# Where a path that is not taken keeps its transfers: GpSimd's queue, and turns on TensorE

## The chip, the cores and the metric

The kernel runs on one core of a Trainium2 chip. The metric is the device time of one execution in microseconds (us), lower is better; the time given for a kernel is the median of its runs. A profile is one more execution, taken with the hardware profiler. It gives a *span*, from the first to the last instruction of the program, which is a little shorter than the device time of that same execution.

The engines are called TensorE (PE, with PEld for its weight loads), VectorE (DVE), ScalarE (ACT), GpSimd (POOL) and SyncE (SP). SyncE computes nothing here; it issues transfers. A name with a q (SPq, ACTq) in a profile means the engine's sequencer: branches, semaphore instructions, drains and the issuing of transfers.

## The reference

The inputs are q, k and v of 4 batches, 8 heads, 768 tokens and 64 channels, a small matrix sort_net of 8x8 for each head, and the weights of a gated block. Cut to what matters:

```python
for _ in range(5):                       # P is sort_net
    P = exp(P - max(P, axis=-1))
    P = P / (sum(P, axis=-1) + 1e-09)
    P = P / (sum(P, axis=-2) + 1e-09)
k_sorted = einsum('bhij,bhjcd->bhicd', P, k_blocks)   # 8 blocks of 96 tokens
v_sorted = einsum('bhij,bhjcd->bhicd', P, v_blocks)
scores = q_block @ k_sorted_block.T / sqrt(64)
attn = softmax(scores)
x = attn @ v_sorted_block                # all heads side by side: 4 x 768 x 512
h = relu(x @ w_in); u, v = halves of h
v_s = w_spatial @ layernorm(v) + b_spatial
out = (u * v_s) @ w_out                  # 4 x 768 x 512, float32
```

## The kernel before, in words

The program has two paths, one after the other. The **usual path** computes everything without the maxima of the reference and without the 1e-09. The **general path** computes all of it again, with the maxima and the small term, one batch after the other and without overlap. It runs only if the usual path met a value outside some bounds. With the inputs used here no value is outside.

The usual path is written as a list of small units (`ORDER`, L18 to L51): `L` loads a q, k or v of one batch, `SK` is one round of the normalisation, `KT` mixes and turns k, `VM` mixes v and `VC` (L415) moves it into blocks, `SC` and `AT` are the scores and the attention of one pair of heads, `XT` (L506) turns attention output on TensorE with four 96x96 transposes a head pair and a copy, `XD` (L497) does the same turn with one transfer that transposes, and so on to `OS` (L643) and `OJ` (L690), which store the output. The list is the order on every engine. The last stores are `OJ` units; each is one transfer on SyncE's queue.

Loads go through GpSimd's queue; `load_sort_net` (L183), `VC`, `XD`, `OS` and `OJ` go through SyncE's. A transfer on SyncE's queue signals one of eight semaphores in turn, each with its own count.

Near the end of the list, `CK` (L694) compares the smallest and largest row sums and column sums with the bounds, `CF` (L709) adds up what it found into one integer, and `LF` (L715) loads that integer into a register of every engine. The branch is the last thing in the program:

```python
with tc.If(st["beyond"] > 0, preferred_fallthrough_block=True, label="general"):
    general_path()
```

Every engine has this branch (L773) in its own list of instructions, behind its last usual unit. An engine that doesn't take the general path jumps over its instructions to a short block of its own. In that block it adds to its semaphores what the general path would have added, each time after waiting that the usual path's own counts are complete, and jumps to the end of the program. There (the line of the launch, L800) SyncE waits for every semaphore in use, twelve instructions with two waits each, and drains; then all engines meet twice, and the program ends.

`general_path` (L724) calls the same unit functions as the usual path, `u_VC`, `u_OS` and `u_XD` among them, so its transfers stand in the queues that those functions name. It uses no `OJ`.

Of the kernel before, what the change touches and what calls it, by code (L numbers as in the profile page):

```python
# [65 lines left out]
def kernel(  # L66
# [12 lines left out]
    nc = tc.nc  # L79

    B, H, S, D = q.shape
# [8 lines left out]
    KC = DM // 128  # L90
    FC = DH // 128
    HP = H // 2
# [12 lines left out]
    def ps_tile(n, dt=FP32):  # L105
        return psum.tile([128, 2, 512 if dt == FP32 else 1024], dt, name=f"ps{n}", tag=f"ps{n}")

    def copy(eng, out, in_):
        if eng == "A":
            nc.scalar.copy(out=out, in_=in_)  # L110
        else:
            nc.vector.tensor_copy(out=out, in_=in_)
# [9 lines left out]
    p_all = const.tile([BH, NB, NB], FP32, name="p_all")  # L122
# [27 lines left out]
    st = {}  # L150
# [30 lines left out]
            nc.gpsimd.dma_start(out=w_out_sb, in_=moe_w_out.rearrange("(fc p) n -> p fc n", p=128))  # L181

    def load_sort_net():  # L183
        nc.sync.dma_start(out=p_all, in_=sort_net.rearrange("b h i j -> (b h) i j"))

    def u_S0():
        load_sort_net()
# [37 lines left out]
    def u_SK(n, safe=False):  # L225
        n = int(n)
        rows, cols = (first[:, 0:NB], first[:, NB:2 * NB]) if n == 0 else (rowsum, colsum)
        over_rows = lambda x: x.to_broadcast([BH, NB, NB])
        over_cols = lambda x: _raw_ap(x, 0, [x.ap[0], [0, NB], x.ap[1]])
        if safe:  # L230
            nc.vector.reduce_max(out=rowsum, in_=p_all, axis=AX.X)
            nc.vector.tensor_sub(out=p_all, in0=p_all, in1=over_rows(rowsum))
        nc.scalar.activation(out=p_all, in_=p_all, func=AF.Exp)
        nc.vector.reduce_sum(out=rows, in_=p_all, axis=AX.X)
        if safe:
            nc.vector.tensor_scalar_add(out=rows, in0=rows, scalar1=1e-9)
        nc.vector.reciprocal(out=rowsum, in_=rows)
        nc.vector.tensor_mul(out=p_all, in0=p_all, in1=over_rows(rowsum))
        nc.vector.reduce_sum(out=cols, in_=p_all.rearrange("p i j -> p j i"), axis=AX.X)
        if safe:  # L240
            nc.vector.tensor_scalar_add(out=cols, in0=cols, scalar1=1e-9)
        nc.vector.reciprocal(out=colsum, in_=cols)
        to = p16.rearrange("p (i j) -> p i j", i=NB) if n == 4 else p_all
        nc.vector.tensor_mul(out=to, in0=p_all, in1=over_cols(colsum))
        if n == 4:
            nc.vector.transpose(out=p_t, in_=p16)

    def u_PR(ps):
        pr = ps_tile(ps)[:, 0, 0:NB * BH].rearrange("p (i y) -> p i y", i=NB)
        for i in range(NB):  # L250
            nc.tensor.matmul(
                pr[:, i, :], lhsT=spread[:, (i % NI) * NB:(i % NI + 1) * NB].rearrange("p j t -> p (j t)"),
                rhs=p_t[:, (i // NI) * BH:(i // NI + 1) * BH], start=True, stop=True,
            )
        st["pr"] = pr
# [6 lines left out]
    def u_P0(lo, hi):  # L262
        lo, hi = int(lo), int(hi)
        n, pr = hi - lo, st["pr"]
        nc.vector.tensor_mul(
            out=pd(0)[:, lo:hi].rearrange("p h (i t) -> p h i t", t=TB),
            in0=_raw_ap(mask16, 0, [mask16.ap[0], [0, n], [0, NB], [1, TB]]),
            in1=_raw_ap(pr, lo, [pr.ap[0], [1, n], [BH, NB], [0, TB]]),
        )

    def u_PC(eng):
        copy(eng, prep_sb, st["pr"])

    def u_PD(b, lo, hi):
        b, lo, hi = int(b), int(lo), int(hi)
        n = hi - lo
        nc.gpsimd.tensor_mul(
            out=pd(b)[:, lo:hi].rearrange("p h (i t) -> p h i t", t=TB),
            in0=_raw_ap(mask16, 0, [mask16.ap[0], [0, n], [0, NB], [1, TB]]),
            in1=_raw_ap(prep_sb, b * H + lo, [prep_sb.ap[0], [1, n], [BH, NB], [0, TB]]),  # L280
        )
# [44 lines left out]
    def u_QN(ps, eng, b, hp):  # L326

        b, hp = int(b), int(hp)
        t = ps_tile(ps).rearrange("p x c -> p (x c)")
        for g in range(G):  # L330
            for hh in range(2):
                nc.tensor.matmul(
                    t[hh * 64:hh * 64 + 64, g * 128:(g + 1) * 128],
                    lhsT=st["q", b][:, 2 * hp + hh, g * D:(g + 1) * D], rhs=ident,
                    start=True, stop=True,
                )
        natural(eng, q_tile(b)[:, hp * S:(hp + 1) * S], t)
# [47 lines left out]
    def u_KT(ps, eng, b, hp):  # L385
        mixed("k", "kT", ps, eng, int(b), int(hp))
# [14 lines left out]
    def u_VM(ps, eng, b, hp):  # L401
        b, hp = int(b), int(hp)
        t = ps_tile(ps)
        for hh in range(2):
            nc.tensor.matmul(
                t[:, hh, 0:G * D], lhsT=pd(b)[:, 2 * hp + hh, :], rhs=st["v", b][:, 2 * hp + hh, :],
                start=True, stop=True,
            )
        copy(
            eng,  # L410
            vm[:, :, 2 * hp:2 * hp + 2, 0:D].rearrange("p g h d -> p h g d"),
            t[:, :, 0:G * D].rearrange("p h (g d) -> p h g d", g=G),
        )

    def u_VC(b, lo, hi):  # L415
        b = int(b)
        for i in range(int(lo), int(hi)):
            nc.sync.dma_start(
                out=vb[b % 2][:, i].rearrange("c h d -> c (h d)"),
                in_=vm[i * TB:(i + 1) * TB].rearrange("t g h d -> t g (h d)"),  # L420
            )
# [75 lines left out]
    def u_XD(b, ih, lo=0, hi=4):  # L497
        b, ih, lo, hi = int(b), int(ih), int(lo), int(hi)
        if ("xT", b) not in st:
            st["xT", b] = att.tile([128, 2, KC, HW], BF16, name="xT", tag="xT", bufs=2)  # L500
        nc.sync.dma_start_transpose(
            out=st["xT", b][:, ih, lo:hi].rearrange("p k (i c) -> p (k i) c", i=NI),
            in_=st["x", b, ih][:, lo:hi].rearrange("p k i c -> p (k i c)"),
        )

    def u_XT(ps, eng, b, ih, lo):  # L506
        b, ih, lo = int(b), int(ih), int(lo)
        if ("xT", b) not in st:
            st["xT", b] = att.tile([128, 2, KC, HW], BF16, name="xT", tag="xT", bufs=2)
        t = ps_tile(ps, BF16)[:, 0, 0:2 * HW].rearrange("p (k i c) -> p k i c", k=2, i=NI)  # L510
        for k in range(2):
            for i in range(NI):
                nc.tensor.transpose(t[:, k, i, :], st["x", b, ih][:, lo + k, i, :], ident[0:BLK, 0:BLK])
        copy(eng, st["xT", b][:, ih, lo:lo + 2].rearrange("p k (i c) -> p k i c", i=NI), t)
# [125 lines left out]
            st["o", b, n0] = ld.tile([128, 3, DM], FP32, name="o_sb", tag="ld")[:, 0:2]  # L640
        copy(eng, st["o", b, n0][:, lo:hi], st["o_ps", b, n0][:, lo:hi])

    def u_OS(b, n0, lo=0, hi=2):  # L643
        b, n0, lo, hi = int(b), int(n0), int(lo), int(hi)
        nc.sync.dma_start(
            out=out[b].rearrange("(c p) n -> p c n", p=128)[:, n0 + lo:n0 + hi, :],
            in_=st["o", b, n0][:, lo:hi],
        )
# [38 lines left out]
        st["o1", b, n, c0] = ld.tile([128, 3, DM], FP32, name="o1_sb", tag="ld")[:, 0, 0:c1 - c0]  # L687
        copy(eng, st["o1", b, n, c0], st["o1_ps", b, n, c0])

    def u_OJ(b, n, c0, c1):  # L690
        b, n, c0, c1 = (int(x) for x in (b, n, c0, c1))
        nc.sync.dma_start(out=out[b, n * 128:(n + 1) * 128, c0:c1], in_=st["o1", b, n, c0])

    def u_CK():  # L694
        nc.vector.memset(bad, 0.0)
# [28 lines left out]
    def general_path():  # L724


        st.clear()
        load_sort_net()
        for n in range(5):
            u_SK(n, safe=True)  # L730
        u_PR(0)
        u_P0(0, 8)
        u_PC("A")
        for b in range(B):
            if b > 0:
                u_PD(b, 0, 8)
            for x in ("q", "k", "v"):
                u_L(x, b, 0, H)
            for hp in range(HP):
                u_VM(2, "A", b, hp)  # L740
            u_VC(b, 0, NB)
            for hp in range(HP):
                u_QN(2, "A", b, hp)
                u_KT(3, "D", b, hp)
                for ih in range(2):
                    u_SM(b, hp, ih)
                    u_AT(2, b, hp, ih)
            for ih in range(2):
                u_XD(b, ih, 0, HP)
            for n in range(0, G, 2):  # L750
                u_VP(n % 4, "A", b, n, n + 1)
                u_ST(b, n)
                u_ST(b, n + 1)
            u_LN(b, 0, G)
            for n in range(G):
                u_LA(b, n)
            for m in range(2):
                for ih in range(2):
                    u_UP(2 * m + ih, "A", b, m, ih)
            for mc in range(FC):  # L760
                u_SP(mc, b, mc)
                u_GT("D", b, mc)
            for n in range(0, G, 2):
                u_OP(n % 4, b, n)
                u_OE("A", b, n)
                u_OS(b, n)
# [38 lines left out]
```

## Time and profile before

| | us |
|---|---|
| median of 3 runs | 161.39 |
| lowest and highest run | 161.30, 161.57 |
| the profiled execution's own time | 161.53 |
| its span | 159.7 |
| TensorE busy | 147.6 |
| VectorE busy | 113.1 |
| ScalarE busy | 85.7 |
| GpSimd busy | 42.2 |

The granted TensorE clock was 0.996 of full speed over the span. Busy times count compute instructions alone; semaphore instructions, branches, drains and the issuing of transfers are not in them, and are seen only when a view is asked for their line. In such an answer a row is: line, sequencer, operation, how many, the duration in ns (smallest, median, largest), and the start of the first and of the last one, in us from the span's start.

### The profile page before, as it was taken

What the parts mean: (1) busy time and instruction counts of PE and PEld (TensorE: products, weight loads), DVE (VectorE), ACT (ScalarE), POOL (GpSimd) and SP (SyncE); (2) the same over time, 40 slices, a digit from 0 to 9 for tenths busy, and PEclk for the clock granted to TensorE, in tenths of its full rate; (3) what the DMA queues carried; (4) which work ended last, traced back from release to release, by engine and by line L of the source; (5) the groups of instructions that cost most, each with busy time, mean ns of one, the idle gap of its engine ahead of it and who ended that gap; (6) DMA issues with size and microseconds to landing.
All of it is one profiled execution on the core that took longest, in us unless ns stands there. A gap on an engine that the chain in (4) does not pass through costs nothing. (4 is left out here: it accounts for less than half of the span.)

```text
span 159.7 us, 3977 instructions
## 1 busy us (share of the span) xinstructions
PE 147.6 (92%) x1647; PEld 89.2 (56%) x1661; DVE 113.1 (71%) x261; ACT 85.7 (54%) x117; POOL 42.2 (26%) x46
## 2 busy tenths in 40 slices
PE   6997989999999999999999999999999999899840
PEld 2355867845686668556465654655655554455410
DVE  4786889638995679867838669897558956947620
ACT  3556799968889409478572446555432242340220
POOL 7942782292000034040000650210004440005300
PEclk9999999999999999999999999999999999999998
DMA  3999999999999999950000657300911377037253
GB/s 84 259 204 204 204 208 202 208 224 239 269 207 202 204 226 241 214 92 4 0 4 0 123 90 131 61 4 0 290 71 34 69 259 266 0 137 259 96 202 112
DMA packets 27526, 23.58 MB, mean 148 GB/s; under 512 B 7280, under 2 KB 24432, under 8 KB 27504
## 3 DMA queue, kind: packets, MB, share of 16 engines
q0 software_dynamic: 14352, 11.80, 46.6%
q1 hardware_dynamic: 13152, 11.49, 25.1%
q8 instruction: 14, 0.23, 0.6%
q14 instruction: 8, 0.07, 0.2%
HBM read 24.78 MB, written 6.29 MB: 195 GB/s over the span
## 5 line engine op out<-in xcount | busy, mean ns | idle before, releaser
L620 POOL TENSOR_TENSOR gt<-z,u_sb 128x768 bf16<-128x768 f32 x10 | 16.4, 1642 | 76.1 <-DVE rec_all L490 55.1
L442 ACT ACTIVATE ex<-ps 96x768 bf16<-96x768 f32 x32 | 24.4, 804 | 7.9 <-PE ps L437 7.8
L604 PE MATMUL ps<-wspT,v_sb 128*128 128x384 bf16 x144 | 25.4, 326 | 0.0
L592 PE MATMUL ps<-xT,w_in_sb 128*128 128x384 bf16 x128 | 23.3, 326 | 0.6 <-ACT o_sb L110 0.6
L491 DVE TENSOR_TENSOR x_sb<-ps,rec_all 96x512 bf16<-96x512 f32 x32 | 22.0, 687 | 1.1
L549 PE MATMUL ps<-w_in_sb,xT 128*128 128x512 bf16 x88 | 21.6, 379 | 0.5 <-issue 0.2
L566 DVE BATCH_NORM_STATS2 stats<-v_sb 128x6 f32<-128x512 bf16 x24 | 16.3, 680 | 5.5 <-ACT v_sb L116 4.3
L610 DVE TENSOR_TENSOR z<-ps,b_bc 128x768 f32<-128x768 f32 x12 | 11.5, 956 | 11.2 <-PE ps L604 11.2
L604 PEld LDWEIGHTS <-v_sb 128*128 128x128 bf16 x144 | 13.3, 98 | 8.4
L116 ACT ACTIVATE u_sb<-ps 128x768 bf16<-128x768 f32 x15 | 12.2, 812 | 10.8 <-PE ps L592 7.9
L116 ACT ACTIVATE v_sb<-ps 128x1024 bf16<-128x1024 f32 (+1 forms) x10 | 9.8, 982 | 14.4 <-PE ps L549 14.4
L592 PEld LDWEIGHTS <-w_in_sb 128*128 128x128 bf16 x128 | 11.8, 98 | 8.7 <-issue 0.9
L630 PE MATMUL ps<-w_out_sb,gt 128*128 128x512 bf16 x68 | 16.3, 379 | 0.2
L110 ACT COPY o_sb<-ps 128x1024 f32<-128x1024 f32 (+1 forms) x10 | 8.4, 839 | 14.7 <-PE ps L680 10.6
L549 PEld LDWEIGHTS <-xT 128*128 128x128 bf16 x96 | 8.9, 98 | 9.8
L483 PEld LDWEIGHTS <-ex 96*128 96x128 bf16 x256 | 10.9, 97 | 3.8 <-DVE x_sb L491 0.3
L483 PE MATMUL ps<-vb,ex 96*128 96x65 bf16 x256 | 12.4, 193 | 0.1
L110 ACT CAST kt<-ps 128x768 bf16<-128x768 f32 x12 | 9.3, 804 | 5.9 <-PE ps L378 5.9
L221 PE MATMUL ps<-warm 128*128 128x512 bf16 x35 | 10.0, 441 | 1.3 <-DVE warm L194 1.3
L630 PEld LDWEIGHTS <-gt 128*128 128x128 bf16 x72 | 6.6, 98 | 7.1
L437 PE MATMUL ps<-qT,kt 64*128 64x96 bf16 x256 | 9.3, 204 | 0.5 <-DVE x_sb L491 0.2
L490 DVE RECIPROCAL rec_all<-ps 96x8 f32<-96x8 f32 x32 | 6.3, 197 | 4.8 <-PE ps L483 4.4
(94 smaller groups left out, 198.5 us busy)
## 6 DMA issues: line engine op xcount, KB each, us to landing
out_dram<-o_sb SPq DMA_DIRECT2D x8, 512.0 KB, 3.7
k_in<-in_k_dram POOLq DMA_DIRECT2D x4, 768.0 KB, 23.9
v_in<-in_v_dram POOLq DMA_DIRECT2D x4, 768.0 KB, 22.8
vb<-vm SPq DMA_DIRECT2D x24, 99.0 KB, 5.6
q_in<-in_q_dram POOLq DMA_DIRECT2D x3, 768.0 KB, 29.0
out_dram<-o_sb SPq DMA_DIRECT2D x7, 256.0 KB, 2.6
ws_in<-in_moe_w_spatial_dram POOLq DMA_DIRECT2D x2, 576.0 KB, 27.8
w_in_sb<-in_moe_w_in_dram POOLq DMA_DIRECT2D x2, 512.0 KB, 23.9
```

The costliest lines, as they stand in the source:

```text
L110: nc.scalar.copy(out=out, in_=in_)
L116: nc.scalar.activation(out=out, in_=in_, func=AF.Relu)
L442: nc.scalar.activation(out=e_tile(b, hp, ih).rearrange("p h (x g) -> p h x g", g=G), in_=t[0:BLK, :, 0:HW].rearrange("p h (g x) -> p h x g ...
L483: nc.tensor.matmul(t[:, hh, ii * VW:ii * VW + D + 1], lhsT=e[:, c:c + 128], rhs=vb[b % 2][:, ih * NI + ii, 2 * hp + hh, 0:D + 1], start=Tr ...
L491: nc.vector.tensor_mul(out=x_sb[:, hp].rearrange("p i (h d) -> p h i d", h=2), in0=tv[:, :, :, 0:D], in1=_raw_ap(rec, 0, [rec.ap[0], [NI, ...
L549: nc.tensor.matmul(t[:, x, :], lhsT=st["xT", b][:, n // 3, kc, (n % 3) * 128:(n % 3 + 1) * 128], rhs=w_in_sb[:, kc, DH:DFF], start=(kc == ...
L566: nc.vector.bn_stats(out=stats, in_=st["v_sb", b, n])
L592: nc.tensor.matmul(t[:, x, 0:HW], lhsT=w_in_sb[:, kc, mc * 128:(mc + 1) * 128], rhs=st["xT", b][:, ih, kc, :], start=(kc == 0), stop=(kc = ...
L604: nc.tensor.matmul(t[:, x, 0:HW], lhsT=st["v_sb", b, n][:, mc * 128:(mc + 1) * 128], rhs=wspT[:, 3 * x:3 * x + 3, n, :], start=(n == 0), s ...
L610: nc.vector.tensor_add(out=z.rearrange("p (x c) -> p x c", x=2), in0=t[:, :, 0:HW], in1=b_bc.rearrange("p (x c) -> p x c", x=2),)
L620: eng.tensor_mul(out=gt, in0=st["z", b, mc], in1=st["u", b, mc // 2][:, mc % 2])
L630: nc.tensor.matmul(t[:, x, :], lhsT=st["gt", b, mc][:, (n0 + x) * 128:(n0 + x + 1) * 128], rhs=w_out_sb[:, mc, :], start=(mc == 0), stop=( ...
```

## The change

A helper `queue` picks the queue of a transfer: GpSimd's once the mark "general" is set, and otherwise the one named (SyncE's by default). `general_path` sets the mark. The calls of `load_sort_net`, `VC`, `OS` and `OJ` ask the helper. In the general path the turn of the attention output is made by `XT`, two head pairs at a time, on TensorE and ScalarE, in place of `XD`'s transposing transfer. The usual path's list is not touched.

```diff
+    def queue(eng):
+        if "general" in st:
+            return nc.gpsimd
+        return nc.scalar if eng == "A" else nc.sync
+
     def load_sort_net():
-        nc.sync.dma_start(out=p_all, in_=sort_net.rearrange("b h i j -> (b h) i j"))
+        queue("S").dma_start(out=p_all, in_=sort_net.rearrange("b h i j -> (b h) i j"))
     def u_VC(b, lo, hi):
         b = int(b)
         for i in range(int(lo), int(hi)):
-            nc.sync.dma_start(
+            queue("S").dma_start(
-    def u_OS(b, n0, lo=0, hi=2):
+    def u_OS(b, n0, lo=0, hi=2, eng="S"):
         b, n0, lo, hi = int(b), int(n0), int(lo), int(hi)
-        nc.sync.dma_start(
+        queue(eng).dma_start(
-    def u_OJ(b, n, c0, c1):
+    def u_OJ(b, n, c0, c1, eng="S"):
         b, n, c0, c1 = (int(x) for x in (b, n, c0, c1))
-        nc.sync.dma_start(out=out[b, n * 128:(n + 1) * 128, c0:c1], in_=st["o1", b, n, c0])
+        queue(eng).dma_start(out=out[b, n * 128:(n + 1) * 128, c0:c1], in_=st["o1", b, n, c0])
         st.clear()
+        st["general"] = True
         load_sort_net()
             for ih in range(2):
-                u_XD(b, ih, 0, HP)
+                for lo in range(0, KC, 2):
+                    u_XT(2 + lo // 2, "A", b, ih, lo)
```

In the built program SyncE then has no transfer in the general path. TensorE has 256 more instructions there, ScalarE 15 more, GpSimd 62 more. The list of the program's inputs starts with sort_net and q, where it started with q and sort_net before.

## The prediction

> **What bounds the kernel now.** I read the page's heading and its busy table first, then the views by line for the lines that only the general path runs, then the chain of work that ended last, and then the sequencers' records of the end, line by line.
>
> ```profile
> span 159.7 us, 3977 instructions
> PE 147.6 (92%) x1647; PEld 89.2 (56%) x1661; DVE 113.1 (71%) x261; ACT 85.7 (54%) x117; POOL 42.2 (26%) x46
> ```
>
> TensorE is busy 92% of the span, so the usual path is bounded by its order on TensorE. Nothing that makes another engine's work shorter would show, unless it lies ahead of the first matmul or behind the last one. The next question is whether any line that the change touches ran at all.
>
> ```profile
> nothing on L231; most used: ['L483', 'L437', 'L378', 'L309', 'L604', 'L592', 'L549', 'L630', 'L513', 'L660', 'L526', 'L221', 'L110', 'L396', 'L680', 'L405', 'L112', 'L442', 'L800', 'L418', 'L490', 'L491', 'L116', 'L566', 'L567']
> p_all<-in_sort_net_dram SPq DMA_DIRECT2D x1, 8.0 KB, 1.6
> ```
>
> Line 231 is the row maximum that only the general path's normalisation takes, and it has no instruction; sort_net is loaded once, where the general path would load it again. So this execution skipped the general path, and every edit of the diff stands in that path (its queue choice answers as before until the mark "general" is set). What is left is how the skipped path shows in an execution that skips it: at the branch, and behind it.
>
> ```profile
> 153.75 0.59 ACT o_sb L110
> 155.43 0.33 SPq L692 DMA_DIRECT2D out_dram<-o_sb  x1
> DMA to landing us min/median/max: 2.4/2.5/2.6
> ```
>
> The chain of work ends with ScalarE's copy at 153.75 + 0.59 = 154.34 us. The timeline has one more issue, the last output transfer on SyncE's queue at 155.43, and the answer for line 692 in the last microseconds says that such a transfer lands 2.4 to 2.6 us after it: at 157.8 to 158.0. The span ends at 159.7. So about 1.7 us at the end hold neither compute nor transfer. Here is what SyncE does in them, from the view of lines 773 (the branch over the general path) and 800 (the end of the program), for SyncE alone, in narrow windows:
>
> ```profile
> L773 SPq EVENT_SEMAPHORE  x6: 17/17/17, 156.0 to 156.4; - x6
> L773 SPq COMPARE_BRANCH  x1: 58/58/58, 155.8 to 155.8; - x1
> ...
> L773 SPq EVENT_SEMAPHORE  x1: 17/17/17, 157.0 to 157.0; - x1
> ...
> L773 SPq EVENT_SEMAPHORE  x1: 17/17/17, 158.0 to 158.0; - x1
> ...
> L800 SPq EVENT_SEMAPHORE  x12: 28/28/28, 158.0 to 158.7; - x12
> ...
> L800 SPq DRAIN  x1: 13/13/13, 158.8 to 158.8; - x1
> 157.96:158.77 0.81, 0.00 (x0) 0.00 (x0) 0.00 (x0) 0.00 (x0) 0.00 (x0) 0.84 0.00 0
> ```
>
> Read it as a queue. The branch is at 155.8. Then come eight semaphore instructions of line 773: six at once (156.0 to 156.4), the seventh at 157.0, the eighth at 158.0. The last two wait for the last transfers; the eighth time is the landing time computed above. Only then come twelve semaphore instructions of line 800, first at 158.0 and last at 158.7, and then the drain at 158.8 that lets all engines meet. The windows row says that from 157.96 to 158.77 no engine works and no byte moves (the last three columns are clock, DMA share and GB/s). That stretch is pure sequencer time behind the last landing, and the change reaches it.
>
> **The change part by part.**
>
> *The counts that the skipped path owes.* Each engine that skips the path pays what the path would have added to its semaphores. A path with transfers on SyncE's queue owes eight counts there, one per semaphore of that queue's transfers, and each of the eight rows above waits first until the usual path's transfers on its semaphore have landed. In the changed program the general path has no transfer on SyncE at all (order of instructions: 35 rows before, 22 after, the 13 of the general path gone), and its skipping block holds for SyncE the jump alone. So the eight rows of line 773 go. GpSimd's block keeps its own number of instructions and adds larger numbers.
>
> *What is late next.* The twelve rows of line 800 stay; they are the end's waits for every semaphore. SyncE now reaches them at 156.0 and not at 158.0. The first four wait for GpSimd's transfers, long landed, and the next eight for SyncE's eight transfers, in the order of the old eight rows. Ten can go at once; at one step each they are done near 156.0 + 10 x 0.06 = 156.6, hidden by the flight of the last transfers. The eleventh takes its semaphore at 157.0, the twelfth at 158.0, and the drain follows one step later.
>
> *The step.* Twelve rows from 158.0 to 158.7 have eleven steps: 0.7 / 11 = 0.064 us each. Before, from the last landing to the drain: one step to the first of the twelve, eleven between them, one to the drain, so thirteen steps, 0.83 us; the windows row brackets the same stretch with 0.81. After: one step. Twelve steps go, 12 x 0.064 = 0.76. From the bracket, 0.81 less one step is 0.75, and I take 0.75. The printed times are rounded to 0.1, so 0.6 to 0.8 could stand for the 0.7; the ends are 0.65 and 0.87, the same 12 steps at 0.055 and 0.073.
>
> *Work that is added in skipped code.* In each of four batches the general path gets 32 turns on TensorE and four copies on ScalarE in place of two transfers that turn, and its transfers are issued by GpSimd. None of it runs here. It makes the stretch longer over which GpSimd's, ScalarE's and TensorE's sequencers jump. The rows of such a jump:
>
> ```profile
> L773 ACTq COMPARE_BRANCH  x1: 50/50/50, 153.8 to 153.8; - x1
> L773 ACTq EVENT_SEMAPHORE  x1: 17/17/17, 156.6 to 156.6; - x1
> ...
> L773 POOLq EVENT_SEMAPHORE  x5: 17/42/43, 150.3 to 150.7; - x5
> L773 POOLq COMPARE_BRANCH  x1: 45/45/45, 149.1 to 149.1; - x1
> L773 POOLq INC_SWDGE_SEM  x1: 508/508/508, 150.8 to 150.8; - x1
> ...
> L773 PEldq COMPARE_BRANCH  x1: 402/402/402, 151.2 to 151.2; - x1
> L773 PEldq EVENT_SEMAPHORE  x1: 51/51/51, 153.7 to 153.7; - x1
> ```
>
> ScalarE needs 2.8 us from its branch to its count at 156.6 (its copy ended at 154.34, so at most 0.6 us of that is the copy, and 2.2 are the jump). SyncE's own jump above took 0.2. The new wait order needs ScalarE's count by 158.0: 1.4 us of cover. GpSimd is done at 150.8 + 0.5 = 151.3, and SyncE asks for it from 156.0 on: 4.7 us of cover, more than a whole jump of 2.8, so even if GpSimd's longer path makes its jump as slow as ScalarE's, nothing is late. TensorE's count at 153.7 has 3.3 us until the eleventh wait at 157.0. I put these at nothing; without cover a jump costs up to 2.8.
>
> [...]
>
> *The usual path's own instructions.* In the order of instructions they are the same on every engine. In the program three units' matmuls of line 483 add their counts once instead of several times, where nobody waited for the counts between: nothing on either side. The list of inputs has sort_net ahead of q, so q may lie elsewhere in memory. No row prices that. The nearest is the spread of the three runs, 161.30 to 161.57, or 0.14 to either side of its middle; I take nothing and keep 0.14 both ways.
>
> *The sum.* The profiled execution took 161.53 with a span of 159.7, so 1.83 us lie around the span and stay. 161.53 - 0.75 = 160.78 for such an execution, with a span of 158.95. It stood 0.14 above the median of 161.39, so the median to expect is 161.39 - 0.75 = **160.64**.
>
> **The rivals.**
>
> *A. The end's waits go under the last flight (the forecast).* For it: 0.81 us without work behind the landing, and the twelve waits need nothing that is late. Its own range: 0.65 to 0.87 saved and 0.14 of spread, 160.4 to 160.9.
>
> *B. Nothing moves.* The 1.83 us around the span would have to take up what the end gives, because something that doesn't depend on SyncE ends last there; or ScalarE's jump becomes 2.1 us longer, so that its count comes at 156.6 + 2.1 = 158.7, just where the twelfth wait stood before. Against: all engines meet after SyncE's drain, so what follows should start earlier with it. It gives 161.4.
>
> [...]
>
> *D. The change doesn't do what it says*: a transfer of the usual path would go to another queue. The usual path asks the new choice before the mark is set and gets SyncE; in the order of instructions its transfers on SyncE are those of before. It would show as another order, and I give it no price beyond B.
>
> **How the numbers follow.** This measurement can tell 0.2%, 0.32 us, from no change. A: 0.77, all of it faster by over 0.2%. B with D: 0.13, within 0.2%. C: 0.10, slower. The likeliest is A, so 160.64. The range begins at A's low end with a little for the inputs' places, 160.35, and reaches over B to 161.5; that leaves out C, and little of A. Faster 0.77, same 0.13, slower 0.10.
>
> **What would show it.** In the changed profile the branch's line should have no semaphore instruction on SyncE; the end's line should have its twelve from 156.0 to 158.0, ten of them by 156.7, and the drain should follow the last landing by one step, not 0.8 us. TensorE's busy time and the issue of the last output should stay at 147.6 and 155.4. [...] If the drain follows the landing at once and the time is still 161.4, B's first form is right. If the last output's issue itself moves by over 0.2 us, something in the usual path changed that I hold to be the same.

## The result, and the profile after

The changed kernel took **160.51 us** (median of 6 runs, 160.36 to 160.54) beside 161.34 us for the kernel before (6 runs, 161.26 to 161.57): a ratio of 0.9944, 95% interval 0.9932 to 0.9956, or 0.83 us less. The forecast was 160.64, 0.75 us less. The changed kernel's profiled execution took 160.36 us with a span of 158.6.

The page of the changed kernel, first its span and busy times:

```profile
span 158.6 us, 3983 instructions
PE 148.5 (94%) x1661; PEld 89.1 (56%) x1661; DVE 113.0 (71%) x261; ACT 85.8 (54%) x117; POOL 42.2 (27%) x46
```

In the busy table the counts are those of before on every engine but TensorE, where 14 records more were caught (each program has 1661 matmuls, as many as weight loads); the extra 0.9 us of busy time goes with them. The heading counts only 6 instructions more, since eight of SyncE's are gone. Now the same end as in the prediction: the chain's last piece and the last issue, then SyncE at the branch (now line 780) and at the program's end (now line 807), in narrow windows:

```profile
153.44 0.59 ACT o_sb L115
155.13 0.33 SPq L697 DMA_DIRECT2D out_dram<-o_sb  x1
...
L780 SPq COMPARE_BRANCH  x1: 58/58/58, 155.5 to 155.5; - x1
...
L807 SPq EVENT_SEMAPHORE  x10: 28/28/28, 155.7 to 156.3; - x10
...
L807 SPq EVENT_SEMAPHORE  x1: 28/28/28, 156.8 to 156.8; - x1
...
L807 SPq EVENT_SEMAPHORE  x1: 28/28/28, 157.6 to 157.6; - x1
L807 SPq DRAIN  x1: 13/13/13, 157.7 to 157.7; - x1
...
157.61:157.67 0.06, 0.00 (x0) 0.00 (x0) 0.00 (x0) 0.00 (x0) 0.00 (x0) 1.00 0.00 0
```

Line 780 has no semaphore instruction on SyncE. Ten of the twelve end waits run at once behind the jump, the eleventh goes with the last landing but one, the twelfth with the last, and the drain follows at once: the windows row, set from the twelfth wait to the drain, is 0.06 us long where the same stretch was 0.81. That is the 0.75.

The two spans differ by 1.1 us. The other 0.3 was there before the end: the last issue stands at 155.1 and not at 155.4. The traces drift apart at 32 us, on TensorE. Before, then after, from the timelines of TensorE:

```profile
32.26 0.38 PE L309 MATMUL ps<-ident,q_in 128*64 128x128 bf16 x7 [0.22 <-issue]
32.57 1.25 PE L549 MATMUL ps<-w_in_sb,xT 128*128 128x512 bf16 x4
```

```profile
31.33 0.98 PE L314 MATMUL ps<-ident,q_in 128*64 128x128 bf16 x24
32.24 1.47 PE L554 MATMUL ps<-w_in_sb,xT 128*128 128x512 bf16 x6
```

In the execution of before TensorE paused for 0.22 us with nothing to wait for ("issue") inside the turn of q, and in that of after it didn't. That belongs to the execution and not to the change: the median difference has 0.08 us beyond the 0.75, not 0.3, and two kernels below with the old end (queues_only, owe_eight) have no such pause and are no faster than before. Among the traces below of kernels with the same usual path, the last issue stands at 155.1 in owe_eight and 155.7 in turns_only, which have the old end, and at 155.6 in owe_seven, which has the new one.

### The profile page after: what moved, and what is told of

The parts are those of the page before. It is cut to its first block, busy times and chain, and to the rows that moved or that the text cites. A ratio compares the mean times of both kernels' runs of the same rounds, so it can differ in the third digit from the quotient of the medians.

```text
span 158.6 us, 3983 instructions
## 1 busy us (share of the span) xinstructions
PE 148.5 (94%) x1661; PEld 89.1 (56%) x1661; DVE 113.0 (71%) x261; ACT 85.8 (54%) x117; POOL 42.2 (27%) x46
## 5 line engine op out<-in xcount | busy, mean ns | idle before, releaser
L554 PE MATMUL ps<-w_in_sb,xT 128*128 128x512 bf16 x96 | 22.6, 379 | 0.0
```

Source lines behind the costliest of these rows:

```text
L554: nc.tensor.matmul(t[:, x, :], lhsT=st["xT", b][:, n // 3, kc, (n % 3) * 128:(n % 3 + 1) * 128], rhs=w_in_sb[:, kc, DH:DFF], start=(kc == ...
```

## The experiments

The kernels of one group ran on one chip beside the kernel before; each ratio is to the kernel before on that chip.

### One part alone

**turns_only** undoes the queues:

```diff
         if "general" in st:
-            return nc.gpsimd
+            return nc.sync
```

> The changed kernel with the general path's transfers back on SyncE's queue and only its turns on TensorE kept. SyncE then owes eight counts again. My theory (what counts is that SyncE's last owed count waits for the last landing, with the end's twelve waits behind it): the gain is gone, 161.3 us, ratio to before 0.999 to 1.001, 0.8 us from the last landing to the drain. Rival 1 (the longer or shorter skipped code, or the turn itself, moved the time): 160.5. Rival 2 (the inputs' places in memory; here q stands first, as in before): 161.3 too, so this run doesn't tell it apart.

Measured: 161.31 us beside 161.29, ratio 1.0004 (0.9993 to 1.0015). **queues_only** undoes the turns:

```diff
-                for lo in range(0, KC, 2):
-                    u_XT(2 + lo // 2, "A", b, ih, lo)
+                u_XD(b, ih, 0, HP)
```

> The changed kernel with the transposing transfers back in the general path: SyncE keeps eight transfers there, one for each of its semaphores, all else is on GpSimd's queue. Sort_net stands first among the inputs, as in the changed kernel. My theory: eight counts owed, so 161.3 us, 0.8 us from the last landing to the drain. Rival (fewer instructions of SyncE's skipped path, or the inputs' places, gave the gain): 160.5.

Measured: 161.48 us beside 161.29, ratio 1.0013 (1.0000 to 1.0025). Each part alone gives nothing; both are needed, because either one leaves SyncE with eight counts to pay. In turns_only the eighth stands at 158.4 and the drain at 159.3. SyncE at the branch of queues_only, whose drain stands at 158.8:

```profile
L779 SPq EVENT_SEMAPHORE  x8: 17/17/17, 156.0 to 158.0; - x8
```

The skipped path held 19 instructions of SyncE here where it held 103, so the shorter jump isn't what was gained.

### Seven counts or eight

**owe_seven** and **owe_eight** put the first 7 or 8 transfers of the general path back on SyncE's queue:

```diff
         if "general" in st:
-            return nc.gpsimd
+            st["general"] += 1
+            return nc.sync if st["general"] <= 7 else nc.gpsimd    # 8 in owe_eight
...
-        st["general"] = True
+        st["general"] = 0
```

> The changed kernel with the first seven transfers of the general path (sort_net and six pieces of the first v move) put back on SyncE's queue, so that SyncE owes seven counts, on every semaphore but that of the last store. q stands first among the inputs, as in before. My theory: the seventh count is paid when the last store but one has landed, about 0.9 us ahead of the last landing; the twelve waits take 12 x 0.064 = 0.77 us and are through just before it. So the gain stays whole: 160.5 us, drain one step behind the last landing. Rival 1 (each owed count costs its share, 0.75 / 8 each): 161.25. Rival 2 (the inputs' places gave the gain): 161.3.

> As owe_seven with one transfer more (the seventh piece of the v move) on SyncE's queue, so that it owes eight counts, the last of them on the semaphore of the last store. My theory: one owed count brings the whole loss back, 161.3 us and 0.8 us from the last landing to the drain, 0.75 us above owe_seven. Rival (each owed count costs its share): within 0.15 us of owe_seven.

Measured: owe_seven 160.59 us, ratio 0.9955 (0.9943 to 0.9967); owe_eight 161.30 us, ratio 1.0006 (0.9996 to 1.0016). One transfer more in a path that doesn't run costs 0.71 us; the seven before it cost nothing that can be measured. SyncE in owe_seven at the branch and at the end (line 808):

```profile
L781 SPq EVENT_SEMAPHORE  x7: 17/17/17, 156.2 to 157.3; - x7
...
L808 SPq EVENT_SEMAPHORE  x12: 28/28/28, 157.3 to 158.2; - x12
L808 SPq DRAIN  x2: 7/10/13, 158.2 to 158.3; - x2
```

And in owe_eight:

```profile
L781 SPq EVENT_SEMAPHORE  x8: 17/17/17, 155.7 to 157.8; - x8
...
L808 SPq EVENT_SEMAPHORE  x12: 27/28/28, 157.9 to 158.6; - x12
```

With seven counts the twelve end waits start at 157.3, when the last transfer but one has landed, and run under the last one's flight; the drain comes with the twelfth at 158.2. With eight they start behind the last landing, at 157.9, and the last of them stands at 158.6. It isn't the number of counts that is paid for, but whether one of them waits for the last landing ahead of the twelve. The seventh is free here because the last two landings lie 0.9 us apart (157.3 and 158.2), a little more than the 0.81 us that the twelve waits took in before.

These four kernels also settle the inputs' places. In the program of owe_seven q stands first, as in before, and it has the whole gain; in that of queues_only sort_net stands first, as in after, and it has none.

### ScalarE's jump and its cover

**act_short** gives copies of the general path to VectorE, so that ScalarE skips 111 instructions:

```diff
-                    u_XT(2 + lo // 2, "A", b, ih, lo)
+                    u_XT(2 + lo // 2, "D", b, ih, lo)
...
-                u_VP(n % 4, "A", b, n, n + 1)
+                u_VP(n % 4, "D", b, n, n + 1)
...
-                u_OE("A", b, n)
+                u_OE("D", b, n)
```

> The changed kernel with 40 of ScalarE's copies in the general path given to VectorE, so that ScalarE's skipped path is 111 instructions long and not 162. In queues_only, where it has 145, the jump took 0.6 us; in the kernel before, with 147, it took 2.8. My theory: the jump falls to 0.6 us, ScalarE's count comes at about 154.1 instead of 156.4, and the time stays at 160.5, because SyncE asks for that count only at 157.6. Rival (the jump was on the path): faster by up to 1 us, 159.5.

Measured: 160.57 us beside 161.24, ratio 0.9951 (0.9935 to 0.9968), the changed kernel's time. ScalarE at the branch in the changed kernel, and then in act_short:

```profile
L780 ACTq COMPARE_BRANCH  x1: 50/50/50, 153.5 to 153.5; - x1
L780 ACTq EVENT_SEMAPHORE  x1: 17/17/17, 156.4 to 156.4; - x1
```

```profile
L780 ACTq COMPARE_BRANCH  x1: 45/45/45, 153.5 to 153.5; - x1
L780 ACTq EVENT_SEMAPHORE  x1: 17/17/17, 154.1 to 154.1; - x1
```

From branch to count it took 2.9 us and now takes 0.6, which is the copy's time: the branch is read while ScalarE's last copy still runs, and that copy ends at 154.0 in the changed kernel and 154.1 in act_short. So 2.4 us of waiting behind the copy fell to nothing, and nothing came of it, since the twelfth wait stands at 157.6 in the changed kernel and 157.9 in act_short. **store_act** takes the cover away: the last stores are reordered, and one goes on ScalarE's queue, ahead of its branch. (Here and below the list is cut to the units that differ.)

```diff
-OJ:3:1:0:512 OJ:3:5:256:512 OJ:3:4:0:512 OJ:3:0:0:512
+OJ:3:1:0:512 OJ:3:0:0:512 OJ:3:5:256:512 OJ:3:4:0:512:A
```

> The changed kernel with its last stores in another order: the columns 0 to 511 of token tile 0, ready earlier, one place ahead, and the store of ScalarE's last copy on ScalarE's own queue. The last issue should come at 154.1 instead of 155.1 and land at 156.6 instead of 157.6. ScalarE's branch now stands behind an issue of 0.3 us, at about 154.4 or as before, and its jump takes 2.8 us, so its count comes between 156.4 and 157.2. My theory: what ends last is now ScalarE's count or the landing, whichever is later, 160.1 us with a count at 157.2, 159.5 with one at 156.6. [...]

**store_act_short** is store_act with act_short's edit.

> store_act with ScalarE's skipped path cut to 111 instructions as in act_short. My theory: the jump no longer stands in the way, the landing at 156.6 ends last and the drain follows one step later: 159.5 us. If store_act was held by ScalarE's jump, this run is faster than it by the jump's excess, up to 0.7 us; if it was held by the landing, they are equal. Rival (the last store goes no earlier): 160.5 in both.

Measured: store_act 160.74 us, ratio 0.9965 (0.9954 to 0.9977), no gain on the changed kernel; store_act_short 159.78 us, ratio 0.9908 (0.9892 to 0.9925), 0.96 us faster than store_act. ScalarE and SyncE's end in store_act, and then in store_act_short:

```profile
L779 ACTq COMPARE_BRANCH  x1: 54/54/54, 154.6 to 154.6; - x1
L779 ACTq EVENT_SEMAPHORE  x1: 17/17/17, 158.1 to 158.1; - x1
...
L806 SPq EVENT_SEMAPHORE  x1: 1067/1067/1067, 157.0 to 157.0; - x1
L806 SPq DRAIN  x1: 13/13/13, 158.1 to 158.1; - x1
```

```profile
L779 ACTq COMPARE_BRANCH  x1: 54/54/54, 154.5 to 154.5; - x1
L779 ACTq EVENT_SEMAPHORE  x1: 17/17/17, 154.9 to 154.9; - x1
...
L806 SPq EVENT_SEMAPHORE  x1: 28/28/28, 156.9 to 156.9; - x1
L806 SPq DRAIN  x1: 13/13/13, 157.0 to 157.0; - x1
```

SyncE's twelfth wait begins at 157.0 in store_act and lasts 1067 ns, until ScalarE's count at 158.1. This is the wait that the prediction held to be covered by 1.4 us, made to happen by taking its cover. The jump took 3.5 us, where 2.8 was expected; what lengthened it no run parts. With the short path the same wait takes 28 ns. So the last stores' order had bought 0.7 us at the landing (156.9 in store_act_short, 157.6 in the changed kernel), and ScalarE's jump had eaten it. Both kernels came out above what was expected, by 0.6 us (160.74 against 160.1) and 0.3 us (159.78 against 159.5); the landing at 156.9 where 156.6 was expected is the second one's 0.3.

### What is left of the branch

**no_branch** leaves out the branch, the general path and the flag's load:

```diff
-GT:P:2:0 LF OS:0:0
+GT:P:2:0 OS:0:0
...
-        with tc.If(st["beyond"] > 0, preferred_fallthrough_block=True, label="general"):
-            general_path()
```

(The unit `BH`, a hint for the branch, goes too.)

> The kernel before without the general path, without the branch and without the load of the flag; it leaves out the general path, so it computes only the usual one. What is left of the branch's cost after the change? My theory: nothing on the path. SyncE goes from its last store straight to the end's waits (nine instead of twelve), waits there for the last landing, and the drain follows one step later: 160.5 us, within 0.2 of the changed kernel. Rival (the branch, the flag's load or the jump still cost something): 160.0 or less.

Measured: 159.17 us beside 161.24, ratio 0.9868 (0.9851 to 0.9886). The theory fell: it gains 2.07 us where the changed kernel gained 0.83, 1.2 us more. In the traces the drain stands at 156.0 and not at 157.7, 1.6 us earlier; 0.3 of that is given back behind it, where the engines' last meeting takes 1.2 us and not 0.9. Of the 1.6, 0.9 is there before the last stores, and comes from the middle of the kernel. VectorE, the flag's load and TensorE in the changed kernel, and then VectorE and TensorE in no_branch:

```profile
132.49 0.18 DVE L572 BATCH_NORM_AGGREGATE mv<-stats 128x2 f32<-128x6 f32 x1
133.78 0.69 DVE L571 BATCH_NORM_STATS2 stats<-v_sb 128x6 f32<-128x512 bf16 x1 [1.10 <-issue]
...
L721 DVEq TENSOR_LOAD <-flag x1: 1185/1185/1185, 132.5 to 132.5; - x1
...
137.81 1.46 PE L597 MATMUL ps<-xT,w_in_sb 128*128 128x384 bf16 x8 [0.66 <-ACT o_sb L115]
```

```profile
132.41 0.18 DVE L567 BATCH_NORM_AGGREGATE mv<-stats 128x2 f32<-128x6 f32 x1
132.51 0.66 DVE L566 BATCH_NORM_STATS2 stats<-v_sb 128x6 f32<-128x512 bf16 x1
...
136.91 1.46 PE L592 MATMUL ps<-xT,w_in_sb 128*128 128x384 bf16 x8
```

The load of the flag into VectorE's register takes 1.2 us between two statistics of the last batch, with 1.1 us of idle time behind it that the profile calls "issue". ScalarE's part of the last normalisation waits for these statistics (3.5 us in the changed kernel, 2.3 in no_branch), its next copy (`o_sb`) stands behind that, and TensorE waits 0.66 us for this copy at 137.8, which it doesn't do in no_branch. So no_branch runs 0.9 us ahead on TensorE from there on, and was less than 0.1 ahead until there. The other 0.7 is at SyncE: in no_branch the last issue stands 0.38 us behind its forerunner (153.15 and 153.53), in the changed kernel 1.08 us (154.05 and 155.13). The changed kernel's last issue but one, and then no_branch's last two in one row:

```profile
154.05 0.63 SPq L697 DMA_DIRECT2D out_dram<-o_sb  x1
```

```profile
153.15 0.83 SPq L692 DMA_DIRECT2D out_dram<-o_sb  x2
```

Three kernels move the flag's load, all with act_short's edit, too. **flag_gap** and **flag_last**:

```diff
-GT:P:2:0 LF OS:0:0
+GT:P:2:0 OS:0:0
...
-OJ:3:5:0:256 OH:1:3:4:0:512:0:4
+OJ:3:5:0:256 LF OH:1:3:4:0:512:0:4      (flag_gap)
-OJ:3:0:0:512
+OJ:3:0:0:512 LF                         (flag_last)
```

> act_short with the load of the flag moved from the middle of the last batch's statistics to a place near the end where every engine waits for TensorE anyway (behind VectorE's first partial output copy). no_branch was 1.3 us faster than the changed kernel, which I did not expect; its trace runs 0.82 us ahead from 137.8 us on, where VectorE's load of the flag (1.2 us at 132.5) stood ahead of the last statistics. My theory: this part, 0.8 us, comes by the move alone: 159.7 us. The pause of 0.455 us behind the 79th record of SyncE's queue stays just ahead of the last store. Rival (the load costs wherever it stands): 160.5.

> act_short with the load of the flag behind the last store on every engine, so that SyncE's three instructions for it follow the last store. In all traces so far SyncE pauses 0.455 us behind its 79th record, whatever it is; here that is the load and no longer the last store but one. My theory: the last issue comes within 0.4 us of the one before, as in no_branch, on top of flag_gap's gain: 159.2 us, equal to no_branch, because everything behind the last issue is under its flight of 2.4 us. Rival 1 (the pause belongs to back-to-back stores, not to a place in the instructions): 159.7, as flag_gap. Rival 2 (load, branch and jump behind the last store outlast the flight): over 159.7.

**flag_last_store** is flag_last with store_act's stores:

> flag_last with the two last stores as in store_act (the earlier one a place ahead, the one of ScalarE's last copy on ScalarE's queue). My theory: the last issue follows ScalarE's copy at once, up to 0.3 us earlier than in flag_last: 158.9 us. Rival (the flight of the last store is not what ends last any more, or two queues hold each other up): 159.2 or more.

Measured, beside 161.17: flag_gap 160.25 us, 0.9939 (0.9927 to 0.9951); flag_last 160.30 us, 0.9939 (0.9927 to 0.9952); flag_last_store 159.99 us, 0.9921 (0.9904 to 0.9939). All three missed. TensorE does run 0.8 us ahead of the changed kernel from 137.8 on in each, so the middle gave what was expected, but the end lost most of it. SyncE's stores at the end of flag_gap:

```profile
L697 SPq DMA_DIRECT2D out_dram<-o_sb x3: 332/554/1130, 152.8 to 155.1; - x3
```

One issue took 1.13 us where 0.33 is usual. In the same stretch runs a transfer that the profile calls "instruction" (a code fetch below) on queue 8. That the queue is TensorE's is my estimate, because it moves most of the code (0.23 MB over the span, against 0.07 on queue 14, in the changed kernel) and TensorE has most of the instructions (3322 of 3983). In the changed kernel the fetch runs from 152.60 to 153.55, TensorE's branch stands at 150.9 and its count at 153.4. That it brings what TensorE jumps to, as the expectation of flag_mid_store below has it, is read from these times alone; no view says whose instructions a queue moves. Here is the row of queue 8 in the view of transfers for 152.1 to 153.6 in flag_gap, and then for 152.6 to 153.6 in the changed kernel; the last column is its share of 16 engines' time in the stretch:

```profile
q8 instruction: 1, 0.02, 6.1%
```

```profile
q8 instruction: 1, 0.02, 5.9%
```

0.061 x 16 x 1.5 us is 1.46 us for that one fetch, against 0.059 x 16 x 1.0 = 0.94. That store and fetch hold each other up is argued from their times alone; no run parts them. The same long issue is in flag_last (1.30 us) and flag_last_store (1.51). In flag_last SyncE's own work behind the last issue also outlasts the flight, its load and then its waits and drain; the twelve waits run without a stop, so none of them waits for a landing:

```profile
L721 SPq TENSOR_LOAD <-flag x1: 691/691/691, 155.5 to 155.5; - x1
...
L807 SPq EVENT_SEMAPHORE  x12: 28/28/28, 157.2 to 157.9; - x12
L807 SPq DRAIN  x1: 13/13/13, 157.9 to 157.9; - x1
```

So rival 2 of its expectation has a part in it. The last kernel has no load at the end, and its longest issue there is 0.68 us. **flag_mid_store** is store_act_short with the load behind the last normalisation of v (unit `LA`), over 13 us ahead of the last stores:

```diff
-GT:P:2:0 LF OS:0:0
+GT:P:2:0 OS:0:0
...
-LA:3:4 LA:3:3 SH:3:3:3:0
+LA:3:4 LA:3:3 LF SH:3:3:3:0
```

> store_act_short with the load of the flag moved behind the last normalisation of v, where VectorE waits 1.26 us for TensorE, and well ahead of the last stores. flag_gap and flag_last gained the 0.84 us in the middle and lost most of it at the end, where one store's issue took 1.1 to 1.3 us, not 0.33, while TensorE's fetch of its jump's target took 1.5 us, not 0.95. My theory: with the load out of the way both in the middle and at the end, all engines' ends move forward together by 0.84 us, nothing new collides, and the time is 159.78 - 0.84 = 158.9 us. Rival (the end loses what the middle gains, wherever the load stands): 159.6 or more.

Measured: **159.09 us** beside 161.21, ratio 0.9873 (0.9857 to 0.9890), 0.69 us below store_act_short's 159.78 (another chip), where 0.84 was expected. TensorE is 0.8 us ahead of store_act_short from 137.8 to the end, and the drain comes 0.8 earlier, at 156.2. VectorE around its load, and SyncE's drain:

```profile
134.99 1.20 DVE L116 COPY o_sb<-ps 128x1024 f32<-128x1024 f32 x1
L720 DVEq TENSOR_LOAD <-flag x1: 544/544/544, 135.7 to 135.7; - x1
136.11 2.02 DVE L582 TENSOR_SCALAR v_sb<-v_sb,mv,rstd 128x512 bf16<-128x512 bf16 x6
...
L806 SPq DRAIN  x1: 13/13/13, 156.2 to 156.2; - x1
```

The load didn't run where VectorE waits for TensorE, as was expected, but at 135.7, while a copy of 1.20 us was under way; it was shorter, too (0.54 us), and VectorE had no idle time by it. This kernel keeps the branch and the general path, and is faster than the kernel before and the changed one; its interval overlaps that of no_branch (0.9851 to 0.9886), which leaves them out.

## Why the prediction was right

*The eight counts go, and the twelve waits go under the flight.* Shown by the changed kernel's trace, row by row, and from the other side by turns_only, queues_only and owe_eight, which bring back the eighth count and the old time.

*Twelve steps of 0.064 us.* The stretch behind the last landing went from 0.81 to 0.06. The time fell by 0.83; owe_seven and act_short, with the same end, fell by 0.70 and 0.67 on their chips. The estimate of 0.75 lies among the three, so how close a single one of them comes to it is in part chance.

*The longer skipped code at nothing.* GpSimd's counts stand at 150.0 to 150.4, 0.3 us earlier like all else in this execution, and ScalarE's count at 156.4, 1.2 us before it is asked for; the prediction had 1.4. What the prediction called cover was cover: act_short brought ScalarE's count 2.3 us forward to no effect, and store_act, without cover, lost what it had won.

*The inputs' places at nothing.* Held, by owe_seven and queues_only.

*The rivals.* B: the 1.8 us around the span stayed (160.36 - 158.6), so nothing there took the gain. C, the slower kernel to which the prediction gives 0.10: no run shows that 15 more instructions make ScalarE's jump slower by its 1.4 us of cover. It took about what it had taken (2.9 us after, 2.8 before), and the longest one seen is store_act's 3.5. There SyncE's twelfth wait does last until ScalarE's count, 1067 ns, as that is late. A jump of 0.6 us over 145 instructions (queues_only) stands beside 2.8 over 147 (before). Queue 14 moved 7 transfers of code in the span of queues_only and 8 in that of before; no view says whose, so what parts the two jumps isn't shown. D: the usual path's counts are unchanged.

*A sign of being wrong that came.* The prediction named a last issue that moves by over 0.2 us as a sign that something in the usual path had changed. It moved by 0.3 in the two profiles. The traces above answer it: the last issue lies between 155.1 and 155.7 with either end, so 0.3 between two executions says nothing of the change.

*One sentence of it was wrong.* "Nothing that makes another engine's work shorter would show, unless it lies ahead of the first matmul or behind the last one." The flag's load on VectorE lies far from both ends and costs 0.8 us on TensorE, as the move in flag_mid_store shows (the load moves on every engine there, but TensorE's lead opens only at 137.8, at the wait that VectorE's load delayed). A sequencer's load counts as no engine's busy time, but the idle time that it leaves does show. In the waits of the kernel before it is this row:

```profile
DVE stats L566 <- issue: 1.1, 1, 1.1
```

The change doesn't touch the load, so the forecast didn't suffer.

## What to carry to other kernels

A path that is skipped isn't free in a program built like this one: it leaves a wait and a count for every semaphore that it would have used (eight on SyncE before the change), and if one of these waits for the last transfer, everything queued behind it comes after the landing (twelve waits here, about 0.75 us). So look at what the issuing engine still has to do when the last byte lands, and keep rarely taken paths off the queue that stores the result. A cover that is measured once (ScalarE's 1.2 us) is spent by the next improvement at that place: ask again which wait comes last.

## What the runs showed of the hardware

ScalarE's jump was short in some kernels and long in others. From branch to count it took 0.6 us over 111 (act_short) or 145 skipped instructions (queues_only), in act_short until the copy that was still running ended (154.1), and 2.8 us over 147 (before). Behind a store and with no copy running, the jump over 111 took about 0.4 us (154.5 to 154.9, store_act_short). Over 162 it took 2.9 us (the changed kernel), so 15 instructions more added next to nothing. It took 3.5 us when a store was issued just ahead of it (store_act). Why it is 0.6 over 145 and 2.8 over 147 no run shows.

SyncE's sequencer paused 0.455 us at one place of its instructions, behind the 79th record, in the traces of this study, whatever stands there: a store in the changed kernel, an end wait in no_branch. In the changed kernel this pause stands ahead of the last store, from 154.68 to 155.13, and so on the path; in before it stands from 154.98 to 155.43. Here are the end waits of no_branch in two windows:

```profile
L798 SPq EVENT_SEMAPHORE  x2: 28/28/28, 154.0 to 154.1; - x2
...
L798 SPq EVENT_SEMAPHORE  x5: 28/28/28, 154.6 to 154.9; - x5
```

Two waits at 154.0 and 154.1, then a pause of half a microsecond, then five more at one step each. Its place goes with the count of records; why, no run shows. A code fetch under way isn't seen beside it everywhere: in the changed kernel one on queue 14 starts at 154.4, takes 0.75 us and ends with the pause, but in no_branch no code fetch starts between 146.2 and 155.5. So the cause is open.

Loading one integer into a register took 0.47 to 1.19 us in the changed kernel and flag_mid_store, and not by engine: VectorE's load took 1.19 us in the changed kernel and 0.54 in flag_mid_store, SyncE's 0.48 and 1.11. Why is open. What it costs depends on what its engine still has to do: between VectorE's short statistics it left 1.10 us of idle time (the changed kernel), under a copy of 1.20 us none (flag_mid_store).
